# A gated linear attention and an MLP on one core: the same turns in another order

## The chip, the cores and the metric

The kernel runs on 1 core of one Trainium2 chip. The metric is the device time of one execution in microseconds (us). Three runs before the change took 424.27, 424.45 and 424.51 us: median 424.45.

The core has five engines, each with an instruction queue of its own that it works off in order. They meet only by semaphores. TensorE (PE; PEld are its weight loads) multiplies matrices and transposes, VectorE (DVE), ScalarE (ACT) and GpSimd (POOL) work element by element, and SyncE (SP) issues nearly all transfers (DMA) of this kernel. SBUF is the memory on the chip that the engines work in, PSUM the banks that TensorE writes to.

## The reference

A recurrence over 768 steps for 4 batches and 8 heads, then an MLP with a residual on what the heads give, laid side by side (4 x 768 x 384):

```python
for t in range(S):
    state = alpha[:, :, t, :, None] * state + np.einsum('bhd,bhe->bhde', k[:, :, t], v[:, :, t])
    y[:, :, t] = np.einsum('bhd,bhde->bhe', q[:, :, t], state)
...
x = np.ascontiguousarray(attn_out.transpose(0, 2, 1, 3)).reshape(B, S, H * D)
...
xn = (x - mu) / np.sqrt(var + 1e-06) * g_ln
ch = np.maximum(xn @ w_ch1, 0.0) @ w_ch2
return (x + ch).astype(np.float32)
```

The inputs q, k, v and alpha are 32-bit floats; the weights w_ch1 (384 x 1536) and w_ch2 (1536 x 384) come as 64-bit floats and are rounded to 32 bits on the core.

## The kernel before, in words

**Tiles and stages.** The sequence is cut into 6 chunks of 128 steps. A chunk of one batch is one piece of attention, 24 in all. Within a chunk the recurrence becomes matrix products: the logarithm of alpha is summed along the steps by a product with a triangle of ones, exponentials of the sums scale q and k, products of the two give scores, and a state of 48 x 48 for each head goes from chunk to chunk. Chunk 0 is worked as a whole, chunks 1 to 5 in two halves. The MLP runs over a chunk of all four batches. Chunk 0 uses plain products (L564 and L576); chunks 1 to 5 use schemes with fewer products (15 for 18 in the first layer, L856; 20 for 24 in the second, L676), whose operands are sums and differences of blocks that VectorE and GpSimd make and whose results they add up.

**What sets the order.** Every piece of work is a generator that issues some instructions and yields; one such step is a turn. A string of 1501 letters, `ORDER`, says which generator has the next turn, and the instructions stand on each engine's queue in just this order. Nothing else schedules. The letters:

- `a` to `x`: the 24 pieces of attention, chunk by chunk and in a chunk by batch (`a` to `d` are chunk 0, `e` to `h` chunk 1, and so on). The turns of one: logarithm of alpha (L296, ACT), its sums (L301, PE, chunk 0), two exponentials (L306 and L307, ACT), the products with q and k (L312, DVE) with the store of the decay row to DRAM (L316, SP), transposes (L328 or L349, PE) and their copies (L333, L335 or L359), scores (L369) and their mask (L379, L380 or L383), the load of the decay gate from that row (L389, SP), the state's update (L399 on PE, L408 or L412 on DVE, L414 on POOL), the output (L424 or L440, PE), its copy (L452, L456, L459), the store of x (L466, SP), the normalization (L470 to L483) and its transposes (L490 or L506) and copies.
- `0`, `1`, `2`, `3`: loads of alpha, k, q and v (L143 to L167, SP). `4` and `5`: sums (L525) and scores (L541) of two batches, chunks 1 to 5.
- `A` to `L`: one of twelve weight pieces each: its load (L214), the rounding on VectorE (L226, L228, L230), one step on ScalarE (L232), the rest of the rounding (L234, L236), and the load of a later piece. Three are in flight.
- `Y`, `Z`: first layer of chunk 0 for two batches each. `P`, `Q`: its second layer (L576, then L580 and the store L555).
- `S`, `W`, `X`, `N`: sums of blocks (L805, L636, L830, L663). `M`, `V`: the products of both layers for chunks 1 to 5 (`V`: the first layer of the last chunk). `R`: the ReLUs (L907). `O`: loads of x for the residual (L551).

**Queues and buffers.** PSUM is one ring of 8 banks: a product whose bank was last read by another engine waits for that engine. SyncE's transfers share eight semaphores in turn, so that a transfer waits until the one eight places ahead has landed, and everything behind it on the queue waits too. The gate's load waits for its row's store in the same queue.

The last 40 matmul groups (the second layer of chunk 5) end the kernel, with the adds and stores behind them.

Of the kernel before, what the change touches and what calls it, by code (L numbers as in the profile page):

```python
# [25 lines left out]


ORDER = (
    "0aa0bb00c2211dd2a3a2aabbbcaaacbbb0bd1a1abbbdfa1dddaaa3bbbec4aac2cd0baaafdAcbe2cc"
    "ffebdddccccdebb31eg0abhAffffeeecA4gdddccA5fdggheddeeeccYYiYhBjfcfhdgeeecggdchhhg"  # L30
    "hBB1ZZZfffB3CCZAefffe5hghB4fCjYYYYYiZZZCYYZZDD2jji3YYiDjjjhiiEZZZC0kDYYY3hhhZEig"
    "FFE5iggjGlF4ZZZZZgglS1lEHYYYhhghHjYYGYYhZZ2llgll3jHZFYGjHkkZkgI0kk0kjjjYZZnKI3i3"
    "ImQSSiiGii4n2jj1jSj5IlkkkkJKSSSSl1feeJn2eKeJLLnhL0hi02jSmPSPSjjmmQ1PPKSSSPkffPP1"
    "fnhPhSmkSWWSQ2SmmSefefWgnggnhQphSogSilllS5n3mimnggXXlXXX33WQQQ0nnXQXk4ppXXomSlll"
    "lnMMpmMoonMMMMMM2MMWSSkk0XSXlmmnnnmmMmMMM3MM13MnMnooppMMMoMMMMWpkrRM0M5poqooo4iq"
    "WWjjMMMMiMMRWMMMpooRiRMMMWMMoMMMlMMOOM1rrr22MMMRRqipMpoiikWMMMMRRMRMMMnnppokMMMM"
    "MRRRNNp3nMONlNlp0nnpWOqtrrmmNWNrN0MMNMMMMMNkNMMMMNN3MMsMMMMMmq0pNlpq1q3kMNOMlkMN"
    "MMMM5XXXXXrrrqq4MqqNXt1XoMMMMMMXXsstqqproM2MrrrJMMuvpoMMMMMMXMMMMMMXsMMMMMtMMrMo"
    "stssMMMqMtMtMM52rrsttssm4ssstMRttMMMMtt1MrMOOMMMMrMvMO2MMMMRRRvRMMMMMMMRRMMRMMML"
    "u31uMMRMRMMssNqNNNvrsmu22RNNNNNRqqNNNNm001MpMMMMMMMMMMM3MMMMMMMMMMMMNMMMrppNoNuv"  # L40
    "vMMoMMMMMXXX3MMM1XXvuu5vuuXvwXXvx4twuuvvqqMXXOOuMMsttttOMMMMMMMMMMXMMMwtMMMMwMMM"
    "33txxxMMMMMMMRqMMMMMMMMMMMMMMMussMsruuwrxRRRMMMMMRRRMRxMMRMMMMwwMMMMMMvxvvvvv5xx"
    "xwwwwwNNRONRRNttqqMMNNxMMMMMxNvMMMMMMMMNNNNNwwxsvMvwwMMxsMMuNNMMXXxNNxxxXXMXXXMM"
    "MXMMMMMXOMMMxMMXXMMMMMMMMMMwwOOuMMMMMMMMMMMMMMMMMMMMMMMMMMMRRRMMMMMMMMMMMROMxwuR"
    "uuwMMMMMMMMMMRRRRNRMMRRMMNMNNMNNNNMMMMMMMMMMMxNMNNXXXXXXMMMXNNMMMMMMNNNMMVVVVVVX"
    "MMMXXXMMMMMMMMVVVVVVVVOOOMOVVVVVVVVVVVVVVVRRRRRVVVVVVVVVRVVVVVVVVVVVVVVVVVVVVVVR"
    "RRNNRNRMMNRNNNMMMNNNMMMMNNNMMMMMMMMMMMMMMMMMMMNNMMMMNMMMMMMMM"
)


# [921 lines left out]
```

## Time and profile before

| what | value |
| --- | --- |
| median of 3 runs | 424.45 us |
| the profiled execution, its own time | 423.99 us |
| its span, first to last instruction | 422.3 us |
| TensorE's granted clock | 1.00 throughout |
| busy: PE / DVE / ACT / POOL | 415.0 / 326.1 / 228.1 / 156.2 us |
| DVE busy from 30 to 56, 56 to 84, 103 to 121 us | 23.57 of 26, 25.71 of 28, 17.09 of 18 us |
| ACT busy from 8.4 to 30, 121 to 141, 141 to 163 us | 19.95 of 21.6, 10.72 of 20, 18.76 of 22 us |
| DMA share from 8.4 to 30, 30 to 56, 278 to 315 us | 0.87, 0.84, 0.15 |
| moved | 43.95 MB in 51159 packets |

A busy TensorE is not TensorE at its peak, since its matmuls are pipelined and their ends are modelled; where it waits is seen from the starts of its instructions and from the chain. The chain is followed back from the last instruction, at each step to what released it. The idle time of an engine that is not in the chain costs nothing.

### The profile page before, as it was taken

Reading aid. Unit: us, or ns where it says so; the run is one execution under the profiler, and the core shown is the slowest. Engines: PE = TensorE matmul, PEld = TensorE weight load, DVE = VectorE, ACT = ScalarE, POOL = GpSimd, SP = SyncE. Lnnn points to the kernel's source line nnn. Section 1 sums busy time; section 2 is a strip of 40 time slices with the busy share of each in tenths; the row PEclk is TensorE's granted clock in tenths of the full one; section 3 lists DMA queues with packets and bytes.
Section 4 is the critical chain, followed back from the end, with each engine's and each line's share of the span. In section 5 each row is a group of like instructions: output and inputs, shape, how many; then the busy total and the mean of one; then the engine's idle time right before and its main releaser. Section 6 shows DMA issues by size and latency. Waiting matters only on the chain.

```text
span 422.3 us, 14142 instructions
## 1 busy us (share of the span) xinstructions
PE 415.0 (98%) x5988; PEld 366.3 (87%) x5988; DVE 326.1 (77%) x626; ACT 228.1 (54%) x572; POOL 156.2 (37%) x181
## 2 busy tenths in 40 slices
PE   7999999999999999999999999999999999999996
PEld 5888878756778889998899998899998899988996
DVE  3599989898998979788669767748676588756684
ACT  5996577969535879344575066496432641124300
POOL 3242010210115590235670334671145650656414
PEclk9999999999999999999999999999999999999999
DMA  7979876883434341251504135002122000130001
GB/s 231 250 204 283 260 182 185 255 241 109 109 109 123 97 153 40 81 143 31 151 17 122 50 97 153 0 22 41 41 86 67 0 2 0 40 113 2 0 20 56
DMA packets 51159, 43.95 MB, mean 104 GB/s; under 512 B 23532, under 2 KB 47212, under 8 KB 51096
## 3 DMA queue, kind: packets, MB, share of 16 engines
q1 hardware_dynamic: 50696, 43.04, 35.3%
q8 instruction: 47, 0.77, 0.8%
q14 instruction: 16, 0.13, 0.1%
q10 hardware_dynamic: 400, 0.00, 0.1%
HBM read 34.29 MB, written 8.74 MB: 102 GB/s over the span
## 4 chain that ended last, share of the span: by engine, by line
PE 93%; ACT 3%; DMA 1%; DVE 1%; issue 1%; SPq 0%; DVEq 0%; ACTq 0%
PE hps L856 31%; PE ops L676 31%; PE ops L576 7%; PE hps L564 7%; PE yps L440 5%; PE aps L541 3%; PE ups L399 2%; PE tps L349 2%; PE lps L525 1%; PE tps L328 1%; DMA rq<-in_q_dram 1%; PE xps L506 1%; ACT at L379 1%; PE xps L490 1%; PE yps L424 0%
## 5 line engine op out<-in xcount | busy, mean ns | idle before, releaser
L692 POOL TENSOR_TENSOR ob<-ob,u 128x192 f32<-128x192 f32 x40 | 25.5, 648 | 88.8 <-DVE ob L689 66.5
L856 PE MATMUL hps<-sum,w 128*128 128x256 f32 x192 | 47.5, 382 | 0.0
L414 POOL TENSOR_TENSOR mid<-mid,gate 112x192 f32<-112x192 f32 x20 | 12.3, 619 | 90.8 <-DVE mid L412 63.2
L856 PEld LDWEIGHTS hps<-sum,w 128*128 128x128 f32 x192 | 36.1, 190 | 4.9
L676 PE MATMUL ops<-w,hT 128*128 128x192 f32 x224 | 39.9, 327 | 0.0
L676 PEld LDWEIGHTS ops<-w,hT 128*128 128x128 f32 x224 | 36.9, 190 | 0.3
L856 PE MATMUL hps<-xT,w 128*128 128x256 f32 x136 | 34.4, 380 | 0.0
L564 PE MATMUL hps<-xT,w 128*128 128x256 f32 x144 | 33.6, 385 | 0.5 <-issue 0.3
L576 PE MATMUL ops<-w,hT 128*128 128x384 f32 x96 | 32.0, 488 | 0.0
L564 PEld LDWEIGHTS hps<-xT,w 128*128 128x128 f32 x144 | 26.5, 190 | 6.0 <-issue 1.5
L907 ACT ACTIVATE hT<-hT 128x512 f32<-128x512 f32 x48 | 27.2, 628 | 7.9 <-POOL hT L894 2.7
L856 PEld LDWEIGHTS hps<-xT,w 128*128 128x128 f32 x136 | 25.8, 190 | 3.5
L676 PE MATMUL ops<-ws,sum 128*128 128x192 f32 x160 | 28.6, 327 | 0.0
L576 PEld LDWEIGHTS ops<-w,hT 128*128 128x128 f32 x96 | 17.9, 190 | 11.5
L686 DVE TENSOR_TENSOR ob<-ops,ob 128x192 f32<-128x192 f32 x50 | 17.1, 352 | 13.2 <-PE ops L676 7.6
L676 PEld LDWEIGHTS ops<-ws,sum 128*128 128x128 f32 x160 | 26.4, 190 | 0.0
L359 ACT COPY qT<-tps 112x512 uint16<-112x512 uint16 x32 | 17.2, 602 | 16.1 <-PE tps L349 16.1
L676 PE MATMUL ops<-ws,hT 128*128 128x192 f32 x128 | 23.4, 326 | 0.0
L510 ACT COPY xT<-xps 128x384 uint16<-128x384 uint16 x32 | 13.5, 491 | 16.3 <-PE xps L506 16.3
L676 PE MATMUL ops<-more,sum 128*128 128x192 f32 x120 | 22.2, 328 | 0.0
L676 PEld LDWEIGHTS ops<-ws,hT 128*128 128x128 f32 x128 | 21.3, 190 | 0.1
L440 PE MATMUL yps<-mid,qT 48*64 48x48 f32 x320 | 21.0, 220 | 0.0
(253 smaller groups left out, 1136.0 us busy)
## 6 DMA issues: line engine op xcount, KB each, us to landing
ws<-in_moe_w_ch_dram SPq DMA_DIRECT2D x12, 768.0 KB, 5.6
vn<-in_v_dram SPq DMA_DIRECT2D x12, 384.0 KB, 3.8
kept<-x SPq DMA_DIRECT2D x20, 192.0 KB, 3.1
ob<-kept SPq DMA_DIRECT2D x20, 192.0 KB, 2.3
out_dram<-ob SPq DMA_DIRECT2D x19, 192.0 KB, 1.9
rq<-in_q_dram SPq DMA_DIRECT2D x16, 192.0 KB, 3.6
rk<-in_k_dram SPq DMA_DIRECT2D x16, 192.0 KB, 3.5
ra<-in_alpha_dram SPq DMA_DIRECT2D x14, 192.0 KB, 3.0
```

The lines of the kernel that those rows point to most:

```text
L359: nc.scalar.copy(out=to, in_=tps[h].bitcast(UINT16).rearrange("r (n p w t) -> r n p t w", n=2, p=NP, w=2)[:R, n])
L414: nc.gpsimd.tensor_mul(new, new, by)
L440: nc.tensor.matmul(yps[r][halves[s], i, p], of, by, start=not (odd and inner), stop=bool(inner or not odd), skip_group_check=bool(odd))
L510: nc.scalar.copy(out=xT_of[c][:, :, b, halves[h]].bitcast(UINT16).rearrange("r f (t w) -> r f t w", w=2), in_=xps[h].bitcast(UINT16)[:, :2 ...
L541: nc.tensor.matmul(aps[halves[i ^ n], p, s], kT[rs, p, s], qT[rs, p, s], start=True, stop=True)
L564: nc.tensor.matmul(hps, w1[:, j // 2, f, j % 2 * P:][:, :P], xT_of[0][:, f, bs], start=(f == 0), stop=(f == NF - 1))
L576: nc.tensor.matmul(ops_of[b], hT_of[c][:, j, b], w2[:, j], start=(j == 0), stop=(j == NJ - 1))
L676: nc.tensor.matmul(acc, lhs[:, j], rhs[:, j], start=(j == 0), stop=(j == NT - 1))
L686: nc.vector.tensor_add(x, acc, x)
L692: getattr(nc.gpsimd, f"tensor_{op}")(x, x, y)
L856: nc.tensor.matmul(acc[:, i], w, b, start=True, stop=True)
L907: nc.scalar.activation(out=x, in_=x, func=AFT.Relu)
```

## The change

Only the string `ORDER` changes. It has the same letters, each as often as before, so each engine gets the same instructions with the same operands and pools, in another sequence. The first lines of the diff:

```diff
 ORDER = (
-    "0aa0bb00c2211dd2a3a2aabbbcaaacbbb0bd1a1abbbdfa1dddaaa3bbbec4aac2cd0baaafdAcbe2cc"
-    "ffebdddccccdebb31eg0abhAffffeeecA4gdddccA5fdggheddeeeccYYiYhBjfcfhdgeeecggdchhhg"
...
-    "RRNNRNRMMNRNNNMMMNNNMMMMNNNMMMMMMMMMMMMMMMMMMMNNMMMMNMMMMMMMM"
+    "0a0b0a0b221d1122cc30aaa1bdacaabbabbbbd2ccabaa1bbc3edd0dAfdaaaca4fcddbcbbaeeebffa"
+    "abgcbddddffcfebc31eeebAhabdccadcAAf23d4gg5ddegchfBfedhheeeccYYYdcdggffgfccgBhhhh"
...
+    "RRMRNNNNRNNNNRNMMMMMNNMMMMMMMMNNMMMMMMMMMMMMNNNMMMMMMMMMMMMMM"
 )
```

What this makes of the queues, at the places that the prediction speaks of:

| place | before | after |
| --- | --- | --- |
| SP, behind four alpha loads, two q loads and two k loads of 192 KB | q, v (384 KB), row `a`, q, row `b`, alpha in three pieces, k, k, gate `b`, row `d`, gate `a`, k, v, row `c`, q (384 KB), alpha in three pieces, first weight piece, q | k, q, q, v (384 KB), alpha in three pieces, row `a`, k, row `b`, q (384 KB), row `c`, gate `a`, k, gate `b`, v, row `d`, alpha in three pieces, first weight piece |
| ACT, at the first L232 | four copies of chunk 1's transposes, L232 | three of them, L232, the fourth (L333 of `f`) |
| DVE, opening | products with q and k: `a`, `b`, `d`, later `c` | `a`, `b`, `c`, `d` |
| DVE near 55 us | L226, L228, L230 of piece `E`, then the add L412 of `h` | the add, then the three |
| DVE near 82 us | L412 of `i` behind L412 of `j`, three steps of `K` and two of `I` | ahead of them |
| DVE near 119 us | the add L412 of `n`, later two of `W` (L636) and one of `X` (L830) | these three, then the add |
| ACT near 138 us | the logarithms (L296) of `q` and `r`, later L470 to L483 of `i` | L470 to L483 of `i`, then the logarithms |
| PE, all | 140 blocks of one line's matmuls; 29 changes from attention to an MLP product, 11 between its layers | 147 blocks; 28 and 19 |

Smaller moves stand at nearly every place of the string; the last 160 matmuls of TensorE are the same.

## The prediction

> **What bounds the kernel now.** I read the page's busy shares and chain first, then the chain in order of time, then the stage in which the chain leaves TensorE.
>
> The page:
>
> ```profile
> span 422.3 us, 14142 instructions
> ...
> PE 415.0 (98%) x5988; PEld 366.3 (87%) x5988; DVE 326.1 (77%) x626; ACT 228.1 (54%) x572; POOL 156.2 (37%) x181
> ...
> PE 93%; ACT 3%; DMA 1%; DVE 1%; issue 1%; SPq 0%; DVEq 0%; ACTq 0%
> ```
>
> TensorE is 98% busy and 93% of the chain; the other 7%, 30 us, is where another order can win. The chain in order of time (start, length, what) shows where:
>
> ```profile
> 2.65 4.98 DMA rq<-in_q_dram
> ...
> 8.44 0.62 PE tps L328 x4
> ...
> 29.92 2.83 PE hps L564 x12
> ...
> 54.92 0.36 DVE mid L412
> ...
> 393.04 26.07 PE ops L676 x160
> ```
>
> The first transposes wait for the first q, which lands at 2.65 + 4.98 = 7.63 us. From 84.47 to 419.16 every piece listed is TensorE. So the first 85 us hold what can be won, and the rest holds what can be lost. In the first stage the VectorE timeline (start, length) shows the rounding of the first weight piece:
>
> ```profile
> 24.24 0.91 DVE L226 TENSOR_SCALAR w<-ws 128x768 int32<-128x768 int32 x1
> 25.18 0.96 DVE L228 SCALAR_TENSOR_TENSOR w<-ws,w 128x768 f32<-128x768 uint32 x1
> 26.17 0.57 DVE L230 TENSOR_SCALAR ws<-ws 128x768 int32<-128x768 int32 x1
> ...
> 27.82 0.96 DVE L234 SCALAR_TENSOR_TENSOR ws<-ws 128x768 int32<-128x768 int32 x1 [0.50 <-ACT ws L232]
> 28.82 0.96 DVE L236 SCALAR_TENSOR_TENSOR w<-w,ws 128x768 f32<-128x768 f32 x1
> ```
>
> L236 ends at 29.78 and TensorE's first MLP product (L564, 29.92) starts at once: this rounding ends last there. Its start follows the weights' landing: SyncE stood 1.2 us for that landing and went on at 24.27. SyncE's waits of the first 30 us:
>
> ```profile
> SPq L147 <- DMA ws<-in_moe_w_ch_dram: 1.2, 1, 1.2
> SPq L160 <- DMA ra<-in_alpha_dram: 1.1, 1, 1.1
> SPq L316 <- ACT eq L306: 0.9, 1, 0.9
> ```
>
> The DMA engines before that landing, in windows of 2 us (last two numbers: share, GB/s):
>
> ```profile
> 10.00:12.00 2.00, 2.00 (x27) 1.78 (x27) 1.82 (x4) 1.97 (x5) 0.00 (x0) 1.00 0.74 204
> 12.00:14.00 2.00, 2.00 (x40) 1.70 (x37) 0.30 (x1) 1.76 (x4) 1.10 (x2) 1.00 0.89 208
> 14.00:16.00 2.00, 2.00 (x76) 2.00 (x73) 1.20 (x4) 2.00 (x6) 1.30 (x3) 1.00 0.90 230
> ...
> 18.00:20.00 2.00, 1.90 (x21) 1.48 (x21) 1.61 (x3) 1.97 (x7) 0.00 (x0) 1.00 1.08 240
> ```
>
> They are full from 18 us on, and left 2 x (0.26 + 0.11 + 0.10) = 0.94 us between 10 and 16 us.
>
> **The change, part by part.** It adds and removes nothing: 1501 turns, each turn with the same instructions, in another order. So every term is a wait or a switch.
>
> *TensorE's own stream.* The build's order gives 29 changes from small attention matmuls to large products before and 28 after; in the rows such a change costs about 0.15 us (L399 to L564, L440 to L856). That is -0.1. Changes between the two MLP layers go from 11 to 19; blocks of L676 ahead of L856 take 162 to 166 ns a matmul against a median of 163, so I price them at 0, at most 8 x 0.05 = +0.4.
>
> *The opening's loads.* SyncE issues in order. Before, the store of batch 0's decay row (L316, turn a) stood ahead of a q load, the alpha pieces and two k loads, and SyncE stood 0.9 us there for the exponential. Now one k load, two q loads, the v load and the three alpha pieces come first. The bytes ahead of the first weight piece are the same (one q load of 384 KB moves forward, but it stood ahead before too), so its landing can gain no more than the hole of 0.94 us and about the 0.9 us wait, and nothing if the hole opens elsewhere: the gates' loads, each behind its row's store, still stand in this queue, and the vector loads behind them. Bounds 0 to -0.9; I take the middle, -0.5. VectorE's 2.1 us wait for k (12.30 to 14.41) is now partly filled by two products of batch 2 (0.55 each), but this does not reach the end of the stage, because the weights' landing comes after it.
>
> *ScalarE behind it.* One copy of 0.59 us (L333, batch 1 of chunk 1) moves behind L232, the rounding's ScalarE step. From there ScalarE ran without a hole to 32.93 (L476), which releases the last normalization for TensorE's transposes of batch 2. If L232 comes no earlier, all of it is 0.5 later; if it comes 0.5 earlier, nothing. Bounds 0 to +0.5; I take +0.2.
>
> L226 took 0.91 us where its twelve have a median of 0.55; it ran while GpSimd masked (L380, 22.80 to 24.73). An earlier start meets the same masks, so up to 2 x 0.36 = 0.7 of the gain may be given back, which lies within the bounds above. The Trainium skill, SBUF — State Buffer, section "SBUF: two separate sides", makes the port pair that these two engines share an exclusive lock, with the later one blocked for the whole of the other's instruction; this trace's 0.91 beside 0.55 agrees, and by that rule the opening's term would be nearer -0.1 than -0.5.
>
> *55 us.* Three rounding steps (L226, L228, L230: 0.55 + 0.96 + 0.56 = 2.07 us) move from ahead of the mid-state add of batch 3 (L412 at 54.92) to behind it. TensorE waited for that add: the weight loads of L564 stood 0.5 us, the matmuls were 0.28 late. Late next is the weight piece of these three steps, whose rounding ended at 60.23 and whose product started at 64.30. -0.3, bounds -0.5 to 0.
>
> *80 to 85 us.* Three adds and one logarithm released TensorE with 0.05 to 0.2 us in hand. One add (batch 0 of chunk 2) moves ahead of six VectorE steps, the last one does not move. -0.2, bounds -0.4 to +0.3.
>
> *VectorE between 30 and 121 us.* Its largest waits in this stretch:
>
> ```profile
> DVE st L412 <- POOL mid L414: 1.9, 3, 0.7
> DVE ws L234 <- ACT ws L232: 1.4, 3, 0.6
> ...
> DVE mid L412 <- PE ups L399: 0.7, 1, 0.7
> ```
>
> The new order puts other work into most of these places: 4.7 us of idle time. It does not set TensorE there, so it is worth 0 itself, but it pays for the next: two combinations of weights (L636, 0.95 each) and one of x (0.42) move ahead of the add of chunk 3, batch 1 (119.00, ends 119.36), which TensorE's first chunk-1 product (120.94) waits for. 2.32 us come ahead of 1.58 us in hand: +0.74 if no idle time is saved, 0 if 0.74 of the 4.7 is. I take 0.
>
> *ScalarE between 121 and 163 us.* Ahead of the two logarithms of chunk 4 now stand the normalization steps of chunk 2, batch 0 (L470, L473, L475, L476, L482, L483: 2.30 us). For batch 1's, 2.88 us come ahead of 1.12 in hand. They are hidden by ScalarE's idle time, in the timeline (start, length):
>
> ```profile
> 133.68 2.05 ACT L359 COPY qT<-tps 112x512 uint16<-112x512 uint16 x4 [3.57 <-PE tps L349]
> ...
> 137.50 0.60 ACT L296 ACTIVATE la<-ra 128x384 f32<-128x384 f32 x1
> ```
>
> The 3.57 us hold 2.88. I take 0; without that cover it is 2.88 - 1.12 = +1.8.
>
> *The end.* The last 40 products (160 matmuls of L676) and what follows are the same: 0.
>
> Sum: -0.1 - 0.5 + 0.2 - 0.3 - 0.2 = -0.9 us on the profiled execution's 423.99 us (422.3 of span and 1.7 around it), 423.1. The median of the three runs is 0.46 above that execution, so against it I say 424.45 - 0.9 = 423.5. What a measurement can tell from no change is 0.2%, 0.85 us: faster means under 423.6, slower over 425.3.
>
> **The rivals.** *All the early idle goes:* the weights land 0.9 earlier, the copy costs nothing, and the waits at 43.45 ("issue", 0.26 in the chain), 55 and 81 to 84 us go whole: -0.1 - 0.9 - 0.3 - 0.5 - 0.4 = -2.2, 422.2. For it: TensorE has no wait after 85 us to lose it in. Against: q and the first weights land by the same bytes. *Nothing that counts changes:* the weights land at 24.2 again, L564 starts at 29.9 again, the later waits change places: 424.2 to 424.9. For it: 93% of the chain is TensorE's unchanged work. *Slower, by ScalarE's backlog at 133 to 140 us:* it decides from the point where less than 1.8 of the 2.88 us finds idle time, for example because the transposes ahead (moved 5 us earlier in TensorE's order) bring the copies of L359 into the same hole. Then the logarithms of chunk 4 are up to 1.8 late, TensorE stands at L525, and nothing behind it can win that back: 423.5 + 1.8 = 425.3, and 424.45 + 1.8 = 426.2 without the early gain. For it: ScalarE is 85% busy from 141 to 163 us (18.76 of 22). Against: 54% from 121 to 141. *That the order is not what ran:* excluded, since the build's order shows other sequences on every engine.
>
> **How the numbers follow.** The forecast (-0.3 to -1.6) gets 0.42, all the early idle 0.12, no change 0.21, the backlog 0.25. The predicted time is the forecast's 423.5; its own range is 422.8 to 424.2. Since cases of both signs hold most of the chance, the range goes from just under the fast rival, 421.9, to between the backlog's two values, 425.7. Faster: the fast rival and 0.33 of the forecast's 0.42, 0.45. Same: the rest of the forecast and no change, 0.30. Slower: 0.25.
>
> **What would show it.** The opening: L226's first start at 23.5 to 24.0 instead of 24.24, and L564's first at 29.2 to 29.8. 55 us: no L412 in the chain there. VectorE: less than 4 us idle between 30 and 121 us. ScalarE: the logarithms of chunk 4 end ahead of L525 with no wait of its weight loads near 139 us. I am wrong if the first L564 starts later than 30.1, or if TensorE waits over 0.5 us anywhere between 85 us and the end.

## The result, and the profile after

| | before | after |
| --- | --- | --- |
| median | 424.36 us (6 runs, 423.16 to 424.51) | 428.79 us (6 runs, 426.64 to 430.01) |
| ratio | | 1.0094, interval 1.0077 to 1.0111 |
| profiled execution, span | 423.99, 422.3 us | 430.01, 428.3 us |
| first L226, first L564 start | 24.24, 29.92 us | 25.31, 32.36 us |
| runs by granted clock | all 1.00 | 1.000: 426.64, 427.49; 0.996: 428.77, 428.82, 429.01; 0.992: 430.01 |

The change made the kernel 0.94% slower by the ratio of the runs, which is not the quotient of the medians (4.43 us, 1.04%); 423.5 had been predicted, in a range of 421.9 to 425.7. The profiled execution is the slowest of the six. From the page of the kernel after:

```profile
span 428.3 us, 14153 instructions
...
PE 419.2 (98%) x5988; PEld 370.5 (87%) x5988; DVE 326.6 (76%) x626; ACT 228.7 (53%) x572; POOL 155.9 (36%) x181
...
PEclk9988999999999999999999999999999999999999
...
PE 91%; DMA 4%; ACT 2%; DVE 1%; SPq 1%; issue 1%; DVEq 0%
```

TensorE's busy time grew by 4.2 us with the same 5988 matmuls, and in slices 3 and 4 of 40 the granted clock reads 8. DMA now has 4% of the chain, 1% before. The chain in order of time (start, length, what) shows the place:

```profile
17.65 7.64 DMA ws<-in_moe_w_ch_dram
...
25.31 1.18 DVE w L226
...
27.98 0.56 DVE xT L493
...
28.59 0.88 PE lps L525 x8
...
32.43 4.69 PE hps L564 x12
```

Before, the weights landed and L236 released L564. Now the chain goes from the weights' landing over the rounding to an L493, a copy that has nothing to do with the weights, and from there to L525. The timelines of TensorE, VectorE and ScalarE there (start, length, what; in brackets the idle time ahead and what ended it):

```profile
23.85 2.07 PE L424 MATMUL yps<-vn,at 128*64 128x48 f32 x64
28.59 0.88 PE L525 MATMUL lps<-la,consts 64*64 64x384 f32 x8 [2.67 <-DVE xT L493]
```

```profile
25.31 1.17 DVE L226 TENSOR_SCALAR w<-ws 128x768 int32<-128x768 int32 x1 [3.52 <-DMA ws<-in_moe_w_ch_dram]
...
27.98 0.55 DVE L493 TENSOR_TENSOR xT<-xps,small 128x384 f32<-128x384 f32 x1
```

```profile
28.11 1.00 ACT L232 ACTIVATE ws<-ws,small 128x768 int32<-128x768 int32 x1 [3.00 <-DVE ws L230]
29.01 0.56 ACT L333 COPY kT<-tps 112x512 f32<-112x512 f32 x1
```

In the kernel before, both L493 stood ahead of the rounding, the L333 ahead of L232, and L525 did not wait:

```profile
23.76 0.56 DVE L493 TENSOR_TENSOR xT<-xps,small 128x384 f32<-128x384 f32 x1 [0.24 <-PE xps L490]
```

```profile
26.07 0.61 ACT L333 COPY kT<-tps 112x512 f32<-112x512 f32 x1
```

```profile
25.40 0.88 PE L525 MATMUL lps<-la,consts 64*64 64x384 f32 x8
```

TensorE of the changed kernel is 1.55 us ahead when the same 274 matmuls lie behind it (23.85 against 25.40 us). Behind the L424 that follow it has nothing to do for 2.67 us. L525 takes a PSUM bank that this L493 frees (batch 1 of chunk 0), and L493 stands on VectorE behind L226, L228 and L230, which wait for the weights. ScalarE too stands 3.00 us, at L232, with the L333 behind it that the next scores (L541) read. What follows the wait is in the windows of 2 us (busy time of PE, PEld, DVE, ACT, POOL; then granted clock, DMA share, GB/s):

```profile
26.00:28.00 2.00, 0.00 (x0) 0.00 (x0) 1.93 (x4) 0.00 (x0) 1.37 (x2) 1.00 0.87 273
28.00:30.00 2.00, 1.38 (x23) 0.85 (x26) 2.00 (x6) 1.90 (x5) 0.00 (x0) 0.85 0.13 32
...
32.00:34.00 2.00, 2.00 (x17) 1.64 (x11) 2.00 (x5) 1.95 (x7) 0.00 (x0) 0.50 0.86 224
...
36.00:38.00 2.00, 2.00 (x25) 1.66 (x27) 0.52 (x1) 0.08 (x1) 0.51 (x1) 0.94 0.35 95
```

From 29.42 us on TensorE had half its clock for 6.83 us. The first twelve L564 took 4.76 us where they took 2.83 before. So of the 6.0 us that the span grew, 2.43 had been lost when L564 started (32.36 against 29.92) and 1.93 more by the end of its twelve matmuls, 4.4 in all within 12 us. Behind that there are single waits: 0.54 at 66.1 and 0.32 at 80.6 ("issue" in the chain), and 1.07 from one start to the next near 300 us, for a sum of blocks (TensorE's only listed wait behind 85 us, here its idle time alone):

```profile
PE ops L676 <- DVE hT L663: 0.7, 1, 0.7
```

### The profile page after: what moved, and what is told of

Read it like the earlier page. It is cut to its first block, busy times and chain, and to the rows that moved or that the text cites. A ratio compares the mean times of both kernels' runs of the same rounds, so it can differ in the third digit from the quotient of the medians.

```text
span 428.3 us, 14153 instructions
## 1 busy us (share of the span) xinstructions
PE 419.2 (98%) x5988; PEld 370.5 (87%) x5988; DVE 326.6 (76%) x626; ACT 228.7 (53%) x572; POOL 155.9 (36%) x181
## 4 chain that ended last, share of the span: by engine, by line
PE 91%; DMA 4%; ACT 2%; DVE 1%; SPq 1%; issue 1%; DVEq 0%
PE hps L856 31%; PE ops L676 29%; PE hps L564 8%; PE ops L576 7%; PE yps L440 5%; PE aps L541 3%; PE ups L399 2%; PE tps L349 2%; DMA ws<-in_moe_w_ch_dram 2%; PE lps L525 1%; DMA row<-eq 1%; PE xps L506 1%; DMA ra<-in_alpha_dram 1%; DMA gate<-row 1%; PE xps L490 0%
## 5 line engine op out<-in xcount | busy, mean ns | idle before, releaser
L907 ACT ACTIVATE hT<-hT 128x512 f32<-128x512 f32 x48 | 28.3, 627 | 21.3 <-POOL hT L878 6.3
L564 PE MATMUL hps<-xT,w 128*128 128x256 f32 x144 | 34.7, 399 | 0.0
L856 PE MATMUL hps<-xT,w 128*128 128x256 f32 x136 | 34.5, 381 | 0.0
L564 PEld LDWEIGHTS hps<-xT,w 128*128 128x128 f32 x144 | 28.2, 200 | 5.0 <-PE aps L541 0.6
L856 PEld LDWEIGHTS hps<-xT,w 128*128 128x128 f32 x136 | 25.6, 190 | 3.4
L676 PE MATMUL ops<-ws,hT 128*128 128x192 f32 x128 | 23.7, 328 | 0.7 <-DVE hT L663 0.7
L440 PE MATMUL yps<-vn,at 64*64 64x48 f32 x320 | 21.2, 219 | 0.5 <-issue 0.5
L440 PE MATMUL yps<-vx,at 64*64 64x48 f32 x320 | 21.3, 219 | 0.0
```

What stands on the lines that cost most here:

```text
L440: nc.tensor.matmul(yps[r][halves[s], i, p], of, by, start=not (odd and inner), stop=bool(inner or not odd), skip_group_check=bool(odd))
L564: nc.tensor.matmul(hps, w1[:, j // 2, f, j % 2 * P:][:, :P], xT_of[0][:, f, bs], start=(f == 0), stop=(f == NF - 1))
L676: nc.tensor.matmul(acc, lhs[:, j], rhs[:, j], start=(j == 0), stop=(j == NT - 1))
L856: nc.tensor.matmul(acc[:, i], w, b, start=True, stop=True)
L907: nc.scalar.activation(out=x, in_=x, func=AFT.Relu)
```

## The experiments

The working theory, called theory 1 in the expectations: TensorE's wait at L525, and the half clock that follows it, are most of the loss. The rivals: the weights' late landing alone (A), a clock that falls by itself (B), a loss spread over later stages (C). In the diffs stand the letters of `ORDER` around the edit; what is the same for long is left out. "Half clock" counts the runs with a granted clock under 0.998; beside the experiments the kernel before had it in 3 of 104. Each ratio is to the runs of the kernel before that were taken beside that run. The starts of L226 and L564 are of one profiled execution, and some of these were far from the median: 429.06 us for e10, 429.11 for e13, 426.22 for e9, 422.88 for e16, 434.84 for e19.

| run | median us | ratio to before | first L226, L564 | half clock |
| --- | --- | --- | --- | --- |
| the changed order | 428.79 | 1.0094 [1.0077, 1.0111] | 25.31, 32.36 | 4 of 6 |
| e5_opening_before | 424.66 | 1.0008 [0.9990, 1.0026] | 23.70, 29.12 | 0 of 12 |
| e2_before_products_late | 425.95 | 1.0049 [1.0031, 1.0066] | 23.52, 31.43 | 3 of 12 |
| e12_before_l333_late | 424.88 | 1.0014 [1.0000, 1.0028] | 23.45, 29.14 | 0 of 12 |
| e1_products_first | 430.41 | 1.0137 [1.0113, 1.0161] | 25.27, 32.02 | 4 of 4 |
| e9_l333_first | 427.59 | 1.0076 [1.0050, 1.0103] | 22.24, 28.88 | 3 of 11 |
| e8_both_copies_first | 427.71 | 1.0091 [1.0064, 1.0118] | 24.88, 30.78 | 5 of 6 |
| e10_rounding_between | 426.49 | 1.0051 [1.0031, 1.0071] | 23.85, 29.91 | 0 of 8 |
| e7_weights_earlier | 432.61 | 1.0187 [1.0153, 1.0221] | 28.97, 34.57 | 5 of 6 |
| e13_weights_in_the_hole | 425.89 | 1.0041 [1.0016, 1.0065] | 26.63, 32.74 | 3 of 12 |
| e15_weights_in_the_hole_2 | 425.74 | 1.0034 [1.0019, 1.0049] | 23.68, 30.30 | 1 of 12 |
| e14_wait_filled | 444.52 | 1.0461 [1.0428, 1.0493] | 22.07, 30.06 | 6 of 6 |
| e16_sums_earlier | 424.58 | 1.0000 [0.9979, 1.0021] | 23.05, 28.76 | 0 of 12 |
| e17_before_long_wait | 425.06 | 1.0016 [0.9993, 1.0039] | 23.00, 30.12 | 2 of 12 |
| e19_before_l564_first | 430.92 | 1.0149 [1.0125, 1.0173] | 24.79, 30.07 | 6 of 6 |

**Where the loss is.** One run, the spliced kernel, has the 135 turns of the kernel before up to its first L564 (`Y`), and then those still to come in the changed order's sequence:

```diff
-0a0b0a0b221d1122cc30aaa1...AAf23d4gg5ddegchfBfedhheeeccYYYdcdgg...
+0aa0bb00c2211dd2a3a2aabb...A4gdddccA5fdggheddeeecc3BfhheYYYdcdgg...
```

> The turns of the kernel before up to the first L564 of chunk 0, and from there the changed order. Theory 1: opening as before (L226 at 24.2, L564 at 29.9, clock 1.0), so only the later waits of the changed order remain (0.7 at 66, 0.5 at 80, 1.0 at 299 us, less about 0.3 at 55): 425 to 426.3. Rival C (the loss is spread over the later stages, the opening is a small part): over 427. If the changed order's later part is the better one: below 424.2.

424.66, ratio 1.0008: between the theory's 425 to 426.3 and no loss at all. The loss is the opening's; the remaining 1366 turns cost nothing that could be measured, their wait of 1.07 us near 295 us included. The waits at 66 and 80 us are not in this trace. Rival C fell.

**Each of the two steps alone, put into the kernel before.** First the rounding (`A`) ahead of the two L493 (`a`, `b`), then L333 (`f`) behind L232 (the second `A`):

```diff
-eg0abhAfff
+eg0hAabfff
```

> The order before the change, with this one part of it added: the two copies L493 of batches 0 and 1 of chunk 0 stand behind L226, L228 and L230 instead of ahead of them. Theory 1: they end at 27.3 and 27.8 instead of 23.5 and 24.3, so that L525 (25.40 before) starts at 27.3 or later, a wait of about 2 us; the next products take L564's place later, so the time is 1.5 to 2.2 above the kernel before, and 1.7 to 3.4 more in runs where the clock falls to half: 426 to 428. Rival A (late landing is the loss): the wait is made up by L564's own wait until 29.8, since that comes behind it anyway: 424.4 to 425. Rival B (clock unrelated): granted clock 1.0 in all runs, time at most 426.6.

```diff
-ffffeeecA4gd
+fffeeecAf4gd
```

> The order before the change, with one part of it added: the fourth copy L333 of chunk 1, batch 1 stands behind L232 and not ahead of it. Theory 1: there the three rounding steps end at 26.74 with the copies done at 26.68, so the copy ends at 28.3 to 28.4, and L541, which starts at 28.21 and needs it a few matmuls later, waits 0.1 to 0.4: 424.3 to 424.8. Rival (the copy behind L232 costs about 2 us wherever it stands): 426 or more. Rival (the ScalarE work behind it, 0.5 later, is what counts): L541 does not wait, but the transposes of batch 2 after L564 do, 424.7 to 425.

The first costs 0.49%, 1.7 us by the medians, just below what was forecast (426 to 428). TensorE's timeline of that run:

```profile
26.61 1.33 PE L525 MATMUL lps<-la,consts 64*64 64x384 f32 x8 [1.59 <-DVE xT L493]
...
31.43 2.86 PE L564 MATMUL hps<-xT,w 128*128 128x256 f32 x12
```

The wait was not made up by L564's own (rival A's 424.4 to 425). The second costs 0.14%, at the edge of what can be told: there the other copies were done before the rounding's three steps ended, and L541 did not wait. Its profile has 1.09 us of "issue" inside an L564 at 43.6 us, where the kernel before has 0.26, so even these 0.5 us need not be the L333's.

**The steps taken back in the changed order.** The rounding behind both L493 (first), only L333 ahead of L232 (second), both (third), and L333 ahead with the rounding between the two L493 (last; each from the changed order):

```diff
-eebAhabdccadcAAf23d
+eebhabdccaAdcAAf23d
+eebAhabdccadcfAA23d
+eebhabdccaAdcfAA23d
+eebhabAdccadcfAA23d
```

> The changed order with one turn moved: the first weight piece's three VectorE steps (L226, L228, L230) stand behind the two copies L493 of batches 1 and 0 of chunk 0, as before the change, and not ahead of them. Theory 1 (TensorE's wait of 2.67 us at 25.9 to 28.6, made by L493 standing behind L226's wait for the weights, and the half clock that follows from it, are most of the loss): L525 starts at 25.9 to 26.1 without a wait; the first L564 then waits for L236 instead and starts at 30.7 to 31.2 (L226 still starts at 25.3), so 1.2 to 1.7 of the 2.67 come off; no half clock, worth another 1.7 on the mean of the runs; time 425.2 to 426.2. Rival A (the weights' late landing, 25.3 for 24.2, is the loss and the wait of L493 only another place for it): L564 starts no earlier than 32, time above 427.5. Rival B (the half clock has nothing to do with TensorE's wait): the wait goes, yet runs still show granted clocks of 0.992 to 0.996, time 426.5 to 427.5.

> The changed order with only the fourth copy L333 moved back ahead of L232; the copies L493 stay behind L226. Theory 1: L525 starts 3.2 to 3.3 behind L226 (three steps of 2.7 and an L493 of 0.55); the wait at L541 is gone. Where the weights land at 25.3 as in the profile of the changed kernel, L525 waits 2.7 and L564 starts at 31.2 to 31.6, 0.8 to 1.1 earlier than there; where they land at 22.5 as in the run before, L525 hardly waits and L564 starts at 28.8 to 29.3. Time between 423.5 (early landing, full clock in all runs) and 428 (late landing). Rival A: L564 at 32 or later, time 428.5 or more.

> The run with the copies L493 ahead of L226 (median 430.41, L226 at 25.27, a wait of 2.29 for the fourth copy L333, L564 at 32.02), and that copy L333 of chunk 1, batch 1 also moved ahead of L232 on ScalarE, as before the change. Theory 1 as it stands now (each of the two steps alone makes TensorE wait for the weights: L525 by L493 behind L226, L541 by L333 behind L232, and whichever is mended leaves the other): no wait at L525 nor at L541; TensorE reaches L564 at 28.9 to 29.2 and waits there for L236, which ends 5.6 behind L226's start; L564 at 30.7 to 31.1 if L226 again starts at 25.3: about 1.0 below that run at equal clock, 428 to 429.5, less where the clock stays full. Rival A (the landing of the weights alone sets L564): L564 at 31.9 to 32.4 as in both runs so far, time 430 or more.

> As the run with both copies ahead, but L226, L228 and L230 stand directly behind the L493 of batch 1 and ahead of the two state updates L408 and the L493 of batch 0. Theory 1: L226 starts at 24.1 to 24.4 if the weights have landed by then (1.0 earlier than behind all of them), L564 5.6 to 5.8 later at 29.7 to 30.2; L525 waits less than 0.3, since only the other batch's L493 stands behind the rounding; time 1.0 below the run with both copies ahead, 426.5 to 428. Rival (the L493 of batch 0 or the L408 hold TensorE as well): L525, L541 or L399 starts behind 27.3 and the time does not fall.

The first was a miss: 430.41, not 425.2 to 426.2. Its L525 did not wait, as forecast, but the scores behind it did. TensorE and ScalarE in that run:

```profile
29.54 1.61 PE L541 MATMUL aps<-qT,kT 48*64 48x64 f32 x59 [2.29 <-ACT kT L333]
```

```profile
28.05 0.97 ACT L232 ACTIVATE ws<-ws,small 128x768 int32<-128x768 int32 x1 [2.77 <-DVE ws L230]
28.92 0.56 ACT L333 COPY kT<-tps 112x512 f32<-112x512 f32 x1
```

So the moved L333, of 0.56 us, held TensorE for 2.29: it stands behind L232, which waits for the rounding. This made theory 1 say "each of the two steps makes TensorE wait for the weights, and what is mended leaves the other". In this trace, though, the weights had landed at 22.5 us. The rounding began at 25.27 because VectorE came to it only behind the L493, for the first of which it stood 1.62 us itself (until 23.59, for TensorE's L490). With both mended the wait went on to L564 (VectorE does the rounding only behind its two L493 and two L408, from 24.88; the weights had landed at 22.4):

```profile
30.78 4.12 PE L564 MATMUL hps<-xT,w 128*128 128x256 f32 x12 [2.65 <-ACT xn L473]
```

L236 ended at 30.64 there, so what ended this wait is the rounding, not the L473 that the line names. 427.71 was just below the forecast of 428 to 429.5; the ratio, 1.0091, is not told apart from the changed order's 1.0094. With the rounding in between L564 stood 1.29 us and started at 29.91, as in the kernel before, at 426.49 (forecast 426.5 to 428). With L333 alone it started at 28.88, 1.04 earlier than before, and yet the median was 427.59 (423.5 to 428, by the landing). What these two lost behind L564 is shown further down.

**What the weights' landing depends on.** The first load's place on SyncE (`A`), ahead of three alpha loads (`0`) instead of behind them, on the run with both L493 ahead of the rounding (430.41):

```diff
-edd0dAfda
+eddA0dfda
```

> As the run with the copies L493 ahead of L226, and besides the first weight piece's load stands on SyncE ahead of the three alpha loads of chunk 1 (384 KB) instead of behind them. Theory 1 with the landing as next limit: the weights land 1.1 to 1.8 us earlier, at 23.5 to 24.2, L226 starts then and L564 at 29.0 to 29.8: another 1.0 to 1.5 below that run, 424 to 425. Rival D (the alpha loads are the next limit): they land up to 3 us later, ScalarE's logarithm L296 of batches 2 and 3 of chunk 1 stands for them with the copies and the masks behind it, and L525 or L564 starts no earlier than in the other run: 425.5 to 427.5.

432.61: rival D, at more than its price. ScalarE's logarithm stood for the alpha that now lands behind the weights, and the copies of scores (L379) behind it held TensorE. The profile also has 1.23 us at L541, 2.41 us of "issue" inside an L564 at 50.3, and two stretches of half clock:

```profile
23.83 0.52 ACT L296 ACTIVATE la<-ra 128x384 f32<-128x384 f32 x1 [3.32 <-DMA ra<-in_alpha_dram]
```

```profile
25.30 0.65 PE L328 MATMUL tps<-consts,qk 128*112 128x128 f32 x4 [2.64 <-ACT at L379]
```

In seven traces with the opening of the kernel before, the weights had landed at 22.7 to 24.8 us. In eight traces with the changed order's loads it was 22.1 to 22.5 in five, and 23.7, 25.3 and 26.6, with the same queue up to there; SyncE issued the load at 16.5 to 18.8, and it was under way for 5.0 to 7.8 us. In the changed kernel's profile eleven of the load's sixteen completion events had come by 22.87, and the last at 25.29: five late ones made the landing late. This profile met one of the late landings, so its wait of 2.67 us need not be that of every execution. What makes the landing vary there was not tried.

**The wait behind L564.** With L333 alone ahead, and with the rounding in between, TensorE stood again, inside one L564, for no semaphore. The timeline of the first of these runs, and its windows with the columns as above:

```profile
41.03 1.13 PE L564 MATMUL hps<-xT,w 128*128 128x256 f32 x4
44.37 0.81 PE L564 MATMUL hps<-xT,w 128*128 128x256 f32 x3 [2.21 <-issue]
```

```profile
40.00:42.00 2.00, 2.00 (x44) 1.30 (x37) 1.78 (x4) 1.40 (x6) 0.00 (x0) 1.00 1.13 371
42.00:44.00 2.00, 0.16 (x1) 0.00 (x0) 2.00 (x4) 1.57 (x4) 0.00 (x0) 1.00 0.91 325
```

The trace's DMA packets have one of 16 KB on the instruction queue from 41.95 to 43.00, and TensorE goes on 1.37 us behind its end. The rounding in between gave the same: packet to 43.74, on at 45.15. The wait sits at the same place of TensorE's stream in the kernel before (0.64 from one start to the next, 43.07 to 43.71, packet to 42.31): at the 725th or 726th matmul in nine of the kernels. If the packet is late because the engines are full of weights, other times for the weight loads move the wait. Both runs got the second and third piece (`B`, `C`) ahead of a decay row (`g`) for which SyncE stands, and the fourth (the second `A` here) ahead of a wait for the second piece's buffer:

```diff
-A23d4gg5ddegchfBfedhheeeccYYYdcdggffgfccgBhhhhfYfZZZfBZeeBef0ijC5e4iCCYYhjghZZZBCYYYADD1
+A23BCd4gg5ddegchffedhhAeeeccYYYdcdggffgfccgBhhhhfYfZZZfBZeeBef0ij5e4iCCYYhjghZZZBCYYYDD1
```

> As the run with the rounding between the two L493 (median 426.49; L564 at 29.91; then a wait of 2.1 to 2.3 inside the L564 of 42.8 to 45.1, for which the profile shows no semaphore, while the instruction queue moves a block of 16 KB from 42.7 to 43.7 and the DMA share is 1.06 and 0.89), with three weight loads earlier on SyncE: the second and third piece directly behind the last v load of chunk 0's order (at about 24.5, ahead of the decay row of chunk 1, batch 2, for which SyncE stands 4.9 us), the fourth behind the decay row of batch 3. Theory F (that wait is for the block of instructions, late because its packet stands behind weight packets): the DMA engines fill the hole of 26 to 30 us and are no longer full at 40 to 44; the wait inside L564 falls below 1.0: 424.4 to 425.4. Rival G (the wait comes from how fast TensorE uses up its instructions, 128 short matmuls in 2 us ahead of it): it stays above 1.8 whatever the DMA does: 426 or more. Rival H (decay rows and gates land late behind the moved loads): waits at L399 or L440 of chunk 1, 427 or more.

> The same three loads moved, on the run that only had the fourth L333 back ahead of L232 (median 427.59, in its profile L564 at 28.88, L525 without a wait since the weights landed at 22.2, and then 2.37 us inside an L564 at 41.8). Theory F: 423 to 424.5 in runs where the weights land at 22.3 and 426 to 427 where they land at 25, so a wider spread than with the rounding in between. Rival G or H: median no lower than 427.

The wait was gone in both, and the engines were idle at that place. In the first the packet was there by 45.69 for a matmul at 47.36, in the second by 41.70 for one at 43.42 (a window of the second):

```profile
40.00:42.00 2.00, 2.00 (x132) 1.85 (x128) 1.93 (x4) 1.94 (x7) 0.00 (x0) 1.00 0.03 8
```

The time followed only in part. From the run with L333 alone 427.59 went to 425.74, between the two forecasts (423 to 424.5 or 426 to 427, by the landing) and so a miss of both. From the run with the rounding between, 426.49 went to 425.89, outside the forecast 424.4 to 425.4; the ratios, 1.0051 and 1.0041, are not told apart. In that run's profile, one of its slowest executions, the weights landed at 26.6, and L541 and L564 waited 1.56 and 1.25 us for what stands behind the rounding. Theory F, that this wait is for a block of instructions that bulk loads make late, holds for this place. In these two runs the packet starts 0.6 us after TensorE has come to the block before it (127 matmuls earlier); in the five traces whose engines were still busy while it moved (share 0.78 to 1.05) it starts 2.5 to 3.6 us after. Rival G, the rate at which TensorE uses up its instructions, fell as the sole cause of this wait, but not in general, as the next run shows.

**The half clock.** A kernel that adds work should tell wait and clock apart. The output products of one batch are issued twice in the changed order, with the same values:

```diff
-        for p in range(NP):
+        for p in [*range(NP)] * (2 if (c, b) == (0, 2) else 1):
```

> The changed order as it is; only the output products L424 of batch 2 of chunk 0 are issued twice in a row (64 matmuls, 2.0 us, the same values again), so that TensorE works through most of the wait that it has in the changed kernel from 25.9 to 28.6. Theory 1 (the half clock follows from TensorE's long wait there): L525 starts where it did, with a wait of at most 0.9, granted clock 1.0 or 0.999 in nearly all runs, and the time is that of the changed order's two runs at full clock, 426.6 to 427.6, against its median of 428.79, although work is added. Rival B (the half clock has nothing to do with the wait): clocks of 0.992 and 0.996 in most runs as with the changed order, 428.5 or more. Rival E (the added products delay the copy of their result on ScalarE or the banks): full clock, but 429 or more.

It failed as a test, at 444.52 us. There was no half clock near 30 us, but the weights had landed at 22.07 in its profile and there was nothing to fill. The 64 more matmuls, 2 us of work, cost 15.7 us against the changed order's median, and 20.2 against the kernel before, by another way. TensorE's timeline and the largest waits of its weight loads in that run (us in total, times, longest):

```profile
40.79 0.63 PE L541 MATMUL aps<-qT,kT 48*64 48x64 f32 x28
45.21 0.80 PE L541 MATMUL aps<-qT,kT 48*64 48x64 f32 x18 [3.79 <-issue]
```

```profile
PEld aps L541 <- issue: 5.6, 4, 3.9
PEld L349 <- issue: 4.3, 4, 2.1
PEld L506 <- issue: 3.4, 6, 1.4
```

All its instructions behind the added ones stand elsewhere in the 16 KB blocks. At the eight longest of these waits (1.2 to 4.0 us, 16.2 in all from start to start) TensorE went on 1.38 to 1.57 us behind the end of such a packet. Seven of them stand among the short matmuls of L541, L399, L349 and L506, which use up a block fastest. Only the first two met busy DMA engines (share 1.03 and 0.63 while the packet moved); at the other six the share was 0.06 to 0.10. So full engines are not needed: a block that is used up in less time than the next one needs to come is enough. One of the six, with its packet from 256.20 to 257.15:

```profile
255.23 1.30 PE L349 MATMUL tps<-consts,qk 64*64 64x64 bf16 x123
258.56 0.24 PE L349 MATMUL tps<-consts,qk 64*48 64x64 bf16 x5 [2.04 <-issue]
```

Three stretches of half clock, of 6.83, 3.41 and 3.41 us, begin beside three of these waits (at 44.80, 92.59 and 259.84).

A long wait without an added instruction was tried in the kernel before. First the two L493 behind all five steps of the rounding, then the first L564 (`Y`) ahead of L525, L424 and L541:

```diff
-eg0abhAffffeeecA4gdddccA5fd
+eg0hAffffeeecA4gdddccAab5fd
```

> The order before the change with the two copies L493 of batches 0 and 1 of chunk 0 behind all five VectorE steps of the first weight piece (L226 to L236) and not only behind three. TensorE stands from about 24.5 to 30 for L525. Theory 1 (the half clock follows from a long wait): granted clock 0.992 or 0.996 in at least three of four runs; first L564 at 34.5 to 35.5, 4.6 to 5.6 later than before; time 424.3 + 5 + 1.7 to 3.4 = 430.5 to 433. Rival B (the clock falls by itself): clocks of 0.999 and 1.0 as in the runs of the kernel before, time 428.5 to 430.

```diff
-ecA4gdddccA5fdggheddeeeccYYiY
+ecAAY4gdddcc5fdggheddeeeccYiY
```

> The order before the change, with the first product L564 of two batches put ahead of L525, L424 and L541 on TensorE (and the two rounding steps L234 and L236 ahead of the state update L408 that stood between). TensorE stands from about 25.4 for the rounding, to about 29.0 to 29.6 (L236 ends 29.78 before, some 0.6 earlier without L408), a wait of 3.6 to 4.2 us with nothing to fill it. Theory 1 (the half clock follows from a long wait): granted clock 0.992 or 0.996 in at least three of four runs, where the kernel before had it in 3 of 93; time 424.4 + 3.6 to 4.2 + 1.7 to 3.4 = 429.5 to 432. Rival B (the clock falls by itself): clocks of 0.999 and 1.0 in nearly all runs, 427.5 to 429.

The first made no long wait: L525 stood 0.57 us for an L408 only, and 425.06 us is within 0.2% of the kernel before. Which bank a product takes follows the order of the turns: since the L493 came behind L525 in it, L525 did not take the banks that they free, and lost the reason to wait for them. The second did it. TensorE's timeline and one of its windows:

```profile
23.34 1.91 PE L328 MATMUL tps<-consts,qk 128*112 128x128 f32 x16
30.07 2.90 PE L564 MATMUL hps<-xT,w 128*128 128x256 f32 x6 [4.82 <-DVE w L236]
```

```profile
32.00:34.00 2.00, 2.00 (x11) 0.56 (x9) 0.00 (x0) 0.00 (x0) 0.00 (x0) 0.50 0.00 0
```

Half clock from 27.74 for 6.83 us, in all six runs under 0.997, 430.92 us as forecast (429.5 to 432). The profile is of the slowest of the six and has other waits as well, 1.19 at 48.7 and 0.83 at 53.4 for blocks of instructions. Rival B fell: with the same instructions the clock falls when TensorE is made to wait. Over all kernels the share goes with the longest wait of TensorE in the one profile of each: 1.6 us or less, 9 of 84 runs (without the kernel before's 3 of 104); 2.0 to 2.3, 7 of 23; 2.6 to 2.7, 14 of 18; 3.8 and more, 12 of 12.

**A wait left in the later part.** The wait near 300 us (295 in the spliced kernel) was taken away by two sums (`N`) moved ahead of two chunk adds (`M`), on the spliced kernel:

```diff
-qNMMMMxxNNMNM
+qNMNNMMMxxMNM
```

> The turns of the kernel before up to the first L564, then the changed order (median 424.66, ratio 1.0008), with two sums of blocks (L663, 0.68 each) moved on VectorE from behind two adds of chunk results (L686) to ahead of them, into 1.41 us in which VectorE stood for a copy L723. Theory 1 (the opening is the loss; of the later waits this one, 1.07 at L676 near 295 us, is the only one above 0.7 there): L676 goes on without a wait there, 423.4 to 423.9, 0.1 to 0.2% below the kernel before. Rival (the adds, 1.36 later, free their banks too late): a wait of about 1 at another L676 of 297 to 303 us, 424.5 or more. Rival (TensorE would stand for the next block or sum anyway): 424.2 to 424.7.

The wait is gone from the trace, but 424.58 is no different from 424.66, with an interval of 0.2% to both sides: a miss of the 0.8 to 1.3 us forecast, and in the range of the second rival, though no other wait of that size stands in its trace. No kernel of the study is faster than the one before beyond its interval.

## Why the prediction was wrong, step by step

*The opening's loads* (-0.5, bounds 0 to -0.9): the step that failed, in its reading of what the landing can do. It priced the landing as the start of the rounding and held that it can gain or change nothing. Neither bound held: against 24.2 us in the kernel before, the weights landed at 22.1 to 26.6 over the traces, and L226 started 1.07 later in the profile. More than that, the step looked on VectorE only at the products of q and k and at L226 itself. It did not name what the new order puts behind L226, that is two L493, nor who waits for these, that is L525. Alone this costs 1.7 us of median (425.95 - 424.28), without any late landing (L226 at 23.52). Part of the wait is the rounding's own: in the changed kernel's profile L226 took 1.17 us, 0.62 over its median before. The prediction had allowed up to 0.7 us for that, beside GpSimd's masks; here a memset of GpSimd (L462, 25.12 to 27.37) ran beside it.

*ScalarE behind it* (+0.2, bounds 0 to +0.5): the same error. The L333 was priced by its 0.59 us for the steps behind it on ScalarE, not by L541, which reads it and stands earlier than those. In the kernel before's order the measured 0.5 us (424.88 - 424.36, interval 0 to 1.2) lies within the price, without a wait at L541; in the changed order it was up to 2.29, because there L232 ahead of it stands 2.77 us for the rounding. The two steps were also added up as if they were independent, though both hang on one rounding: mending one leaves the other's wait, and mending both leaves L564's, even where the weights have landed 2.5 us before the rounding begins.

*The clock* was no step at all. The table before the prediction had 1.00 throughout, and the sum let every stall cost its own length. Here a stall of 2.7 us cost up to 3.4 more (two windows of 3.41 us at half clock lose half of 6.83). In the changed kernel's own runs it is 1.8 us from clock 1.000 to 0.996 (means 427.07 and 428.87) and 1.1 more to 0.992. The Trainium skill, TensorE: Matmul & The Clock Gate, section "Part 1: The HAM clock gate", lets the clock fall to 4/8 after at least one idle window of about 3.4 us and has the windows run freely. The lengths of 3.41 and 6.83 us here agree, and so does the variation from run to run; but an idle time of 2.67 us, shorter than a window, was enough in the profiled run. At full clock the changed kernel is 2.7 us above the one before (427.07 from two runs, against 424.36), and the opening carries that too, since the rest is worth 1.0008. There is no trace of those two runs: which of the waits they met stays open.

*TensorE's own stream* (-0.1): not told apart; the spliced kernel, with most of these switches, is not told apart from the kernel before. *55 us* (-0.3): right in what it named, no L412 stands in the chain from 50 to 90 us. *80 to 85 us* (-0.2): not shown: the chain of the kernel before has TensorE alone there and no add, so there was little to win, and 0.32 us of "issue" came in.

*VectorE between 30 and 121 us* (0): right value, wrong reason. The idle time was to fall under 4 us; it is 8.7 (91 - 82.27 busy), where it was 7.3. TensorE did not wait for the moved add, nor did it in the spliced kernel, which comes to it without the opening's delay. *ScalarE between 121 and 163 us* (0) and the rival of its backlog: no wait of L525 near 139 us, and 0.3 us in all for an L296 elsewhere in this stretch. The slower rival had the right sign at the wrong place, by another mechanism: its sign was luck. *After 85 us:* the sign of error named, a wait over 0.5 us, came true near 300 us, but taking it away gained nothing that could be measured. The other, L564 behind 30.1, is the one that told.

## What to carry to other kernels

When an instruction that waits for a transfer is moved forward on an in-order engine, list everything that it overtakes and who waits for each of those, PSUM banks included: a copy of 0.5 us then costs as much as the transfer is late. Price the transfer's landing as a range from several traces, not as the one that the profile shows; a stage that ran with 1.55 us more in hand was worth nothing as long as the next stage waits for that landing. And a stall of TensorE of more than 2 us has a second price in its clock, which may be as large as the first.

## What the runs showed of the hardware

Blocks of instructions can be late. TensorE's instructions come in packets of 16 KB through the DMA engines (47 packets for 11976 matmuls and weight loads). In all traces, every wait of TensorE that the profile puts down to "issue" (29 of 0.17 to 3.79 us, in thirteen kernels) ended 1.27 to 1.60 us behind the end of such a packet. Two things make such a wait: engines full of other loads, which make the packet start late (share 1.13 and 0.91 with the wait at L564, 0.03 without), and short matmuls, which use up a block before the next can come, with engines at 0.06 to 0.10 as well. 64 more matmuls put other work at the edges of the blocks, so that eight such waits cost 16 us. The Trainium skill, Runtime: NRT & Kernel Launch, section "Instruction fetch mechanics", describes refills in 16 KiB blocks and calls the price of a boundary mostly hidden; the size agrees, but in streams of short matmuls (128 in 2.0 us) it is not hidden here.

The half clock came in lengths of 3.41 and 6.83 us only, apart from the last us of the traces. In the nine cases with one wait beside it, in six kernels, it began between 2.3 us before the end of the wait (the one of 4.82 us) and 1.4 behind it (the one of 2.65). In a tenth there were only two waits of 1.56 and 1.25 us.
